# Two seventh token chunks, one per block, joined into one wide output group

## The chip, the core and the metric

The kernel runs on one core of a Trainium2 chip. Its engines work side by side, each through its own queue in program order: TensorE multiplies matrices (its weight loads are listed apart), VectorE and ScalarE do elementwise work and empty the accumulators (PSUM), GpSimd does elementwise work on SBUF and issues the loads, SyncE issues the stores. They wait for each other through semaphores. The metric is the device time of one execution in microseconds (us): 421.94 us for the kernel before, as the median of three runs.

## The reference

The inputs are q, k and v of shape (8, 12, 448, 64) and the three weights of a gated feed-forward block. In numpy:

```python
attn = softmax(q @ k.T / 8) @ v            # per batch and head
x    = attn.transpose(0, 2, 1, 3).reshape(3584, 768)
g    = x @ w_gate                          # 768 -> 1536
val  = x @ w_val
out  = (g * sigmoid(g) * val) @ w_out      # 1536 -> 768, float32
```

Everything before the final output is held in float16 on the chip, with float32 accumulation.

## The kernel before

**Blocks.** The 3584 tokens fall into four groups of two batches, 896 tokens each (`kk` = 0 to 3). While attention runs, the feed-forward work of groups 0 and 1 fills TensorE between attention's products. Groups 2 and 3 are put off to the end. They are the last two stages of the kernel, called here the first and the second put-off block. Each has two parts.

**The hidden part (`Unit`, L883, and `unit_items`, L1400).** The activations `hts` have the layout [128, 12 feature blocks, 896 tokens], in one buffer that both put-off blocks use in turn. A unit makes two feature blocks of gate (even unit `u`) or value (odd `u`) for all 896 tokens by a Strassen-Winograd scheme: seven products P1 to P7 of three matmuls each, instead of eight. Sums of the weights come from GpSimd (`weight_sums`, L873) and sums of the tokens from VectorE. A1 and A2 are ScalarE copies; D1 and D2 are VectorE additions (L964 and L968); F00, F01, F10 and F11 are the four outputs. For a value unit the F's run on VectorE (L982) and write `hts`: F00 and F10 write tokens 0 to 447 of the lower and the upper feature block of the pair, F01 and F11 write tokens 448 to 895. There are 12 units, `u` = 0 to 11.

**The output part (`OutPair`, L770).** A group of 896 tokens has seven chunks of 128. Chunks 0 to 5 form three pairs. `wide` (L800) computes a pair's 256 output rows by seven products again: a pair's activations are split into x and y (its two chunks) and into the lower and upper six feature blocks, so a11 and a12 are the halves of x, a21 and a22 those of y. Each product is six matmuls of 384 columns, with weights from `wo` or their sums `Tsum`. The products are taken in this order: a11; a21 + a22; s2; a12; s3; s4; a22. The four sums come from `h_sums` (L588 to L598) on VectorE: s3 = a11 - a21 (L593); a21 is overwritten by a21 + a22 (L594); s2 = a21 - a11 (L595); s4 = a12 - s2 (L596). Each of the four handles 128x768 elements. s2, s3 and s4 lie in one of three places, `Hall[0]` to `Hall[2]`. `add_sum` pops the next sum from a list, four during each `wide`, so that each pair's sums run during the pair before it. The first pair of a block has no pair before it, so its four sums are items of the hidden part (H0 to H3).

Chunk 6 has no partner. `single_out` (L1108) computes it plainly: 12 feature blocks times two halves of the output columns, 24 matmuls of 384 columns (items O0_0 to O1_11), a ScalarE copy per half (L1114) and a store per half.

**What sets the order.** `order_of` (L44) plans each put-off block. Items have an engine, a cost in us and a list of items that must be done. The planner repeatedly takes the engine whose next item can start first, and of that engine's items that can start within 0.12 us of that moment the one that stands first in the list. Instructions are emitted in that order, and each engine runs its own in the order of emission. The O and H items stand last in the list. After the planned items come the three `wide` calls of the block (`run_wide`, L1467), and after the first block's three pairs the second block's plan.

**Buffers.** `vraw` held the v inputs. Seen flat as `vfree`, its slots 6 to 8 (`vfree[:, 6 * VE :]`, 1536 elements per partition) hold one of the first put-off block's token sums (t6[1], which P6 reads) until that block's units are done. GpSimd's last work is the weight sums of unit 11.

Of the kernel before, what the change touches and what calls it, by code (L numbers as in the profile page):

```python
# [10 lines left out]
FP32 = mybir.dt.float32  # L11
FP16 = mybir.dt.float16
AF = mybir.ActivationFunctionType
# [3 lines left out]
HS = 4096.0  # L17
# [22 lines left out]
PE_, ACT_, DVE_, POOL_ = "PE", "ACT", "DVE", "POOL"  # L40
# [25 lines left out]
def kernel(  # L66
# [10 lines left out]
    nc = tc.nc  # L77
    B, H, S, D = q.shape
# [5 lines left out]
    NFB = DF // 128  # L84
# [5 lines left out]
    OH = DM // 2  # L90
# [23 lines left out]
    ps_f = ctx.enter_context(tc.tile_pool(name="ps_f", bufs=2, space=PSUM))  # L114
# [24 lines left out]
    NH = NFB // 2  # L139
# [12 lines left out]
    def hview(lo, n):  # L152
        return hall[:, ds(lo * NFB, n * NFB)].rearrange("p (f t) -> p f t", t=n)

    wo_all = consts.tile([128, 2, NFB, OH], FP16, name="wo")
    wo = [wo_all[:, i] for i in range(2)]
# [428 lines left out]
            lambda: nc.vector.tensor_sub(t4, b21, t2),  # L585
        ]

    def h_sums(hts, t, at, eng=nc.vector, f0=0, n=NH):  # L588
        lo, hi, x, y = ds(f0, n), ds(NH + f0, n), ts(2 * t, 128), ts(2 * t + 1, 128)
        a11, a12, a21, a22 = hts[:, lo, x], hts[:, hi, x], hts[:, lo, y], hts[:, hi, y]  # L590
        s2, s3, s4 = (h[:, lo] for h in Hall[at])
        return [
            lambda: eng.tensor_sub(s3, a11, a21),  # L593
            lambda: eng.tensor_add(a21, a21, a22),  # L594
            lambda: eng.tensor_sub(s2, a21, a11),  # L595
            lambda: eng.tensor_sub(s4, a12, s2),  # L596
        ]

    class Step:
        def __init__(self, kk, c0, n, hts, fb, late=None):  # L600
            self.at, self.hts, self.fb, self.late = (kk, c0, n), hts, fb, late
            self.t1 = None
            self.split = self.alone = False
            self.time = NCB * n / 2400.0
# [101 lines left out]
    def store(osb, kk, l0, n, m0, w, queues=(nc.sync,), large_first=False):  # L706
        parts = []
        l = l0
        while l < l0 + n:
            b, j = divmod(l, S)  # L710
            turned = D if b + NB * kk < QUAD // NHP else 0
            c, p0 = divmod((j + turned) % S, P)
            m = min(P - p0, l0 + n - l, (MQ if turned and j < MQ else S) - j)
            dst = out[ts(NB * kk + b, S), :].rearrange("(p c) m -> c p m", c=NC)[c, p0 : p0 + m]
            parts.append((m, dst[:, ds(m0, w)], osb[l - l0 : l - l0 + m, ds(m0, w)]))
            l += m
        if large_first:
            parts.sort(key=lambda part: -part[0])
        for x, (_, dst, src) in enumerate(parts):
            queues[x % len(queues)].dma_start(dst, src)  # L720
# [25 lines left out]
    def new_osb():  # L746
        return fp.tile([128, DM], FP32, tag="osb", bufs=4, name="osb")
# [21 lines left out]

    class OutPair:  # L770
        def __init__(self, kk, c0, hts, t, at=None, last=False):
            self.kk, self.c0, self.hts, self.t, self.last = kk, c0, hts, t, last
            self.at = t if at is None else at
            self.x, self.y = ts(2 * t, 128), ts(2 * t + 1, 128)
            self.osb = None

        def sums(self):
            return h_sums(self.hts, self.t, self.at)

        def hh(self, half, z):  # L780
            return lambda n: self.hts[:, half * NH + n, z]

        def hs(self, m):
            return lambda n: Hall[self.at][m][:, n]
# [10 lines left out]
            return self.osb  # L795

        def stored(self, z, lo=0, w=DM, queues=(nc.sync,)):
            store(self.osb[z], self.kk, self.c0 + (2 * self.t + z) * 128, 128, lo, w, queues, self.last)

        def wide(self, keep, add_sum, ns=(1, 2, 1), units=()):  # L800
            osb = self.open()
# [202 lines left out]
    with tc.manual_schedule():  # L1004
# [46 lines left out]
        sums = []  # L1051
# [52 lines left out]
        def token_space(flat, w):  # L1104
            n = min(4, flat.shape[1] // (NK * w))
            return [flat[:, ts(j, NK * w)].rearrange("p (c q) -> p c q", c=NK) for j in range(n)]

        def single_out(op, kk, c0, hts, ch, half, f):  # L1108
            nc.tensor.matmul(  # L1109
                op, lhsT=hts[:, f, ts(ch, 128)], rhs=wo[half][:, f], start=f == 0, stop=f == NFB - 1  # L1110
            )
            if f == NFB - 1:
                osb = new_osb()
                nc.scalar.activation(osb[:, ts(half, OH)], op, AF.Copy, scale=1.0 / HS)  # L1114
                store(osb, kk, c0 + ch * 128, 128, half * OH, OH)

        def add_sum(n=1):
            for _ in range(n):
# [77 lines left out]
        for kind in OPENING:  # L1196
            n = nth[kind]
# [29 lines left out]
        last = len(units)  # L1227
        while g < last or queue:
            n = 2 if g < WIDE * NC else 3
# [29 lines left out]
        vfree = vraw[:].rearrange("p s h c d -> p (s h c d)")  # L1259
        VE = 2 * NC * D  # L1260
# [4 lines left out]
        for x, (chunks, todo) in enumerate(plan):  # L1265
# [73 lines left out]
            if 0 < base - x <= len(FIRST_STEPS):  # L1339
                n = FIRST_STEPS[x - base]  # L1340
# [99 lines left out]
        def run_items(items):  # L1440
            items = {n: (e, t, [a for a in after if a in items], fn) for n, (e, t, after, fn) in items.items()}
            for name in order_of(items):
                items[name][3]()

        hts = hview(0, NT)

        def units_of(kk, t, last):
            units = {}
            items = unit_items(units, lambda u: Unit(u, S, X[kk], t, hts), S)
            pairs = [OutPair(kk, 0, hts, p, p if last else p % 2, last and p == 2) for p in range(3)]  # L1450
            ops = []

            def single_last(half, f):
                if not f:
                    ops.append(ps_f.tile([128, 512], FP32, tag="f", name="op")[:, 0:OH])
                single_out(ops[half], kk, 0, hts, 6, half, f)

            for half in range(2):
                for f in range(NFB):
                    after = [f"F{f % 2}1_{f // 2 * 2 + 1}", f"O{half}_{f - 1}" if f else f"F10_{NFB - 2 + half}"]  # L1460
                    items[f"O{half}_{f}"] = (PE_, OH / 2400 + 0.0025, after, lambda half=half, f=f: single_last(half, f))
            for m, fn in enumerate(pairs[0].sums()):
                u = NFB - 1 if m else NH - 1
                items[f"H{m}"] = (DVE_, 0.65, [f"F00_{u}", f"F10_{u}"] + [f"H{m - 1}"] * (m > 0), fn)
            return items, pairs

        def run_wide(pairs):  # L1467
            for n, pair in enumerate(pairs):
                pair.wide(kept[2 * (n % 2) : 2 * (n % 2) + 2], add_sum)

        items, pairs = units_of(KL - 1, t6, False)
        p0 = NPAIR - 1
        pv_open(p0, True)
# [11 lines left out]
            items[f"W_{u}"] = (POOL_, 3.65, [f"W_{u - 1}"], lambda u=u: weight_sums(u))  # L1485
        run_items(items)

        t7 = token_space(xp.tile([128, NCB, NT], FP16, tag="X", name="T")[:].rearrange("p a b -> p (a b)"), S)
        sums.clear()
        sums.extend(f for pair in pairs[1:] for f in pair.sums())  # L1490
# [4 lines left out]
        for t in qk16s:  # L1495
            flat = t[:].rearrange("p t c h d -> p (t c h d)")
            Hall[2].append(flat[:, 0 : NH * 128].rearrange("p (c f) -> p c f", c=NH))
        items, pairs = units_of(KL, t7, True)
        run_items(items)

# [32 lines left out]
```

## Time and profile before

| what | us |
|---|---|
| three runs, median (lowest, highest) | 421.94 (421.89, 422.28) |
| the profiled execution, its own time | 421.66 |
| its span, first to last instruction | 419.9 |
| TensorE busy / VectorE / ScalarE / GpSimd | 413.5 / 270.0 / 247.8 / 224.4 |
| first put-off block: last unit's last product begins, wide pairs begin | 318.94, 323.08 |
| second put-off block: the same | 391.36, 395.50 |
| the 24 matmuls of one chunk 6: 2 before the last product, 22 after it | 0.33 + 3.58 |
| one wide pair (42 matmuls), from pair to pair in the second block | 6.83 |

Times in the profile are microseconds from the span's start. A line of the timeline gives start, duration, engine, source line, operation, the tensors out<-in, shapes and a count; in brackets stands how long the engine had been idle and what released it. Matmuls are pipelined: a 384-column matmul is listed with 326 ns but the next one starts 0.1625 us after it, a 448-column one with 352 ns and 0.189 us. L numbers are lines of the kernel above; `un` and `ub` are the accumulators of the hidden part, `op` those of chunk 6, `og` and `ob` those of the wide pairs.

### The profile page before, as it was taken

How to read it: one execution, taken by the hardware profiler on the slowest of the kernel's cores; microseconds unless marked ns; L12 is line 12 of the kernel's file. 1: busy time of each engine (PE TensorE's matmuls, PEld its weight loads, DVE VectorE, ACT ScalarE, POOL GpSimd, SP SyncE). 2: the span in 40 equal slices, each digit the busy share in tenths (PEclk: the TensorE clock that was granted, in tenths of full speed). 3: DMA queues.
4: the chain of work that ended last, by engine and by line, in shares of the span. 5: the costliest groups of instructions: out<-in, count | busy, mean ns of one | idle time of the engine just before them, and what ended most of it. 6: DMA issues, size and time to landing. Idle time of an engine off the chain costs nothing.

```text
span 419.9 us, 10841 instructions
## 1 busy us (share of the span) xinstructions
PE 413.5 (98%) x4340; PEld 259.5 (62%) x4340; DVE 270.0 (64%) x614; ACT 247.8 (59%) x386; POOL 224.4 (53%) x343
## 2 busy tenths in 40 slices
PE   8999999999999999999999999999999999999996
PEld 3666666655567786787768676545555655555564
DVE  4767562785687784676746568665755665665563
ACT  6975667656677675787647676645453125555221
POOL 8656624997798986497987806599700000000000
PEclk9999999999999999999999999999999999999999
DMA  8999999999999999999999734600001240000125
GB/s 133 188 200 200 200 174 195 144 154 196 180 185 138 147 219 175 153 152 161 152 179 164 105 72 90 186 14 0 2 0 30 85 118 33 0 2 0 39 75 152
DMA packets 108467, 50.29 MB, mean 120 GB/s; under 512 B 60416, under 2 KB 105344, under 8 KB 108416
## 3 DMA queue, kind: packets, MB, share of 16 engines
q0 software_dynamic: 46800, 24.56, 49.3%
q1 hardware_dynamic: 61344, 24.79, 33.5%
q8 instruction: 34, 0.56, 0.6%
q10 hardware_dynamic: 272, 0.25, 0.2%
q14 instruction: 17, 0.14, 0.1%
HBM read 49.55 MB, written 11.01 MB: 144 GB/s over the span
## 4 chain that ended last, share of the span: by engine, by line
PE 94%; DVE 2%; ACT 1%; DMA 1%; issue 1%; SPq 0%; DVEq 0%
PE gp L610 14%; PE un L915 12%; PE vp L610 12%; PE og L759 10%; PE ub L915 10%; PE acc L462 8%; PE ob L759 8%; PE s L356 5%; PE op L732 4%; PE s L393 2%; PE acc L426 2%; PE op L1109 2%; PE s L368 1%; PE tp L324 1%; ACT E L403 1%; DMA rk<-in_k_dram 1%
## 5 line engine op out<-in xcount | busy, mean ns | idle before, releaser
L378 ACT ACTIVATE E<-s 128x896 f16<-128x896 f32 x126 | 107.5, 917 | 37.4 <-PE s L356 27.3
L610 PE MATMUL gp<-X,wg 128*128 128x256 f16 (+3 forms) x396 | 61.7, 302 | 0.0
L610 PE MATMUL vp<-X,wv 128*128 128x256 f16 (+3 forms) x396 | 58.6, 291 | 0.0
L180 POOL DMA_DIRECT2D vraw<-in_v_dram x72 | 43.9, 632 | 18.1 <-DMA wo<-in_moe_w_out_dram 8.3
L240 POOL COPY qk<-qkraw 128x512 f16<-128x512 f16 x70 | 43.0, 661 | 18.7 <-DMA qkT<-qk 18.2
L610 PEld LDWEIGHTS <-wv 128*128 128x128 f16 x438 | 41.1, 98 | 15.2 <-DVE xt L505 0.2
L180 POOL DMA_DIRECT2D qkraw<-in_k_dram x70 | 42.6, 625 | 5.2 <-DMA wo<-in_moe_w_out_dram 3.4
L403 ACT ACTIVATE E<-s 112x896 f16<-112x896 f32 x48 | 40.6, 917 | 7.5 <-PE s L393 7.5
L610 PEld LDWEIGHTS <-wg 128*128 128x128 f16 x396 | 34.9, 98 | 16.2 <-issue 2.2
L462 PEld LDWEIGHTS <-E 128*128 128x128 f16 (+2 forms) x1224 | 38.1, 98 | 9.1 <-issue 3.9
L462 PE MATMUL acc<-vo,E 128*128 128x65 f16 (+2 forms) x1224 | 42.1, 193 | 0.6 <-DVE osb L816 0.3
L759 PEld LDWEIGHTS <-hts 128*128 128x128 f16 x270 | 25.9, 98 | 16.0
L690 DVE SCALAR_TENSOR_TENSOR t<-sg,gp 128x384 f32<-128x384 f32 (+1 forms) x30 | 18.0, 615 | 24.0 <-ACT sg L637 23.8
L696 DVE SCALAR_TENSOR_TENSOR hts<-t,vp 128x256 f16<-128x256 f32 (+3 forms) x66 | 30.7, 465 | 3.4 <-PE vp L610 1.2
L505 DVE TENSOR_TENSOR xt<-acc,R 128x256 f16<-128x256 f32 x72 | 30.6, 425 | 2.5
L203 POOL DMA_DIRECT2D qkraw<-in_q_dram x43 | 29.4, 684 | 4.0 <-DMA vraw<-in_v_dram 1.1
L356 PE MATMUL s<-qkT 64*64 64x448 f16 (+1 forms) x288 | 28.8, 352 | 0.0
L980 ACT ACTIVATE silu<-un 128x448 f32<-128x448 f32 x24 | 13.0, 543 | 22.4 <-PE un L915 21.8
L964 DVE TENSOR_TENSOR un<-ub,kept 128x448 f32<-128x448 f32 x24 | 15.1, 630 | 16.1 <-ACT kept L961 10.3
L759 PE MATMUL og<-wo,hts 128*128 128x384 f16 x132 | 25.0, 326 | 0.0
L968 DVE TENSOR_TENSOR kept<-ub,kept 128x448 f32<-128x448 f32 x24 | 15.0, 625 | 14.7 <-PE ub L915 14.7
L221 DVE COPY vo<-vraw 128x512 f16<-128x512 f16 (+1 forms) x48 | 21.1, 440 | 2.9 <-DMA vraw<-in_v_dram 2.9
(210 smaller groups left out, 735.4 us busy)
## 6 DMA issues: line engine op xcount, KB each, us to landing
vraw<-in_v_dram POOLq DMA_DIRECT2D x72, 64.0 KB, 5.3
qkraw<-in_q_dram POOLq DMA_DIRECT2D x39, 112.0 KB, 4.9
qkraw<-in_k_dram POOLq DMA_DIRECT2D x68, 64.0 KB, 5.1
wg<-in_moe_w_gate_dram POOLq DMA_DIRECT2D x8, 288.0 KB, 10.2
wv<-in_moe_w_val_dram POOLq DMA_DIRECT2D x8, 288.0 KB, 10.5
wo<-in_moe_w_out_dram POOLq DMA_DIRECT2D x2, 1152.0 KB, 18.7
out_dram<-osb SPq DMA_DIRECT2D x7, 288.0 KB, 3.5
out_dram<-osb SPq DMA_DIRECT2D x9, 192.0 KB, 3.2
```

Of the source, the lines that this page charges most:

```text
L180: eng.dma_start(dst[ts(s, 64)], rows)
L203: nc.gpsimd.dma_start(dst, flat.rearrange("h (p c) d -> p h (c d)", c=NC))
L240: nc.gpsimd.tensor_copy(dst.rearrange("p c h d -> p h c d"), src)
L356: nc.tensor.matmul(s[ts(half, m), hx, 0:S].rearrange("p (c q) -> p c q", q=P), lhsT=t[ts(hx, 64), ds((c + low(pr, hx)) * 128 + half * m, m ...
L378: nc.scalar.activation(e, s[:, :, 0:S], AF.Exp, scale=sm_scale)
L403: nc.scalar.activation(e[:, :, 0:S], s[0:P, :, 0:S], AF.Exp, scale=sm_scale)
L462: nc.tensor.matmul(acc[ds(lo, m), ts((j + pr % 2) % (KR + 1), D + 1)], lhsT=e[rows, ds(hx * S + j * 128 + lo, m)], rhs=Vts[pr % NV][rows, ...
L505: nc.vector.tensor_tensor(xt[:, :, hx], a4[:, :, 0:D], r[:].unsqueeze(2).to_broadcast([128, KR + 1, D]), ALU.mult,)
L610: nc.tensor.matmul(dst[:, 0:w], lhsT=wslice(kind, self.fb, cb), rhs=X[kk][:, cb, ds(c0 + lo, w)], start=(cb == 0), stop=(cb == NCB - 1),)
L696: nc.vector.scalar_tensor_tensor(self.hts[:, self.fb, ds(lo, w)], self.t1[:, ds(lo, w)], 0.5 * HS, vp[:, 0:w], ALU.mult, ALU.mult)
L759: nc.tensor.matmul(dst, lhsT=lhs(n), rhs=rhs(n), start=first and n == 0, stop=n == NH - 1, skip_group_check=True)
L915: mm = nc.tensor.matmul(dst, lhsT=lhs[:, n], rhs=rhs[:, n], start=first and n == 0, stop=n == NK - 1, skip_group_check=True,)
```

## The change

Chunk 6 of neither block is computed alone any more. When the first put-off block's units are planned and emitted, GpSimd copies its chunk 6 (all 12 feature blocks, 128x1536 elements) from `hts` into the free slots of `vraw` (`apart_chunk`). The second block then has four wide groups: its first pair, a mixed group with x = the kept chunk and y = its own chunk 6, and its other two pairs. The mixed group's two output tiles go to the rows of their own blocks. The mixed group's sums run during the first pair's `wide`, like any pair's; the third place for sums, used by the last pair before, now belongs to the pair of chunks 2 and 3, and the last pair uses the first place.

In both put-off blocks the first pair's sums H1 to H3 are planned in two parts: feature blocks 0 to 3 of each half ("e", which need the F's up to unit 9) and 4 to 5 ("l", which need unit 11). H0 stays whole. The removed O items leave the plan without TensorE work behind the last product.

```diff
-    def h_sums(hts, t, at, eng=nc.vector, f0=0, n=NH):
-        lo, hi, x, y = ds(f0, n), ds(NH + f0, n), ts(2 * t, 128), ts(2 * t + 1, 128)
-        a11, a12, a21, a22 = hts[:, lo, x], hts[:, hi, x], hts[:, lo, y], hts[:, hi, y]
+    def h_sums(x, y, at, eng=nc.vector, f0=0, n=NH):
+        lo, hi = ds(f0, n), ds(NH + f0, n)
+        a11, a12, a21, a22 = x[:, lo], x[:, hi], y[:, lo], y[:, hi]
...
     class OutPair:
         def __init__(self, kk, c0, hts, t, at=None, last=False):
-            self.kk, self.c0, self.hts, self.t, self.last = kk, c0, hts, t, last
-            self.at = t if at is None else at
-            self.x, self.y = ts(2 * t, 128), ts(2 * t + 1, 128)
+            self.last, self.at = last, t if at is None else at
+            self.rows = [(kk, c0 + (2 * t + z) * 128) for z in range(2)]
+            self.x, self.y = (hts[:, :, ts(2 * t + z, 128)] for z in range(2))
...
-            pairs = [OutPair(kk, 0, hts, p, p if last else p % 2, last and p == 2) for p in range(3)]
-            ops = []
...
-            for half in range(2):
-                for f in range(NFB):
-                    after = [f"F{f % 2}1_{f // 2 * 2 + 1}", f"O{half}_{f - 1}" if f else f"F10_{NFB - 2 + half}"]
-                    items[f"O{half}_{f}"] = (PE_, OH / 2400 + 0.0025, after, lambda half=half, f=f: single_last(half, f))
-            for m, fn in enumerate(pairs[0].sums()):
-                u = NFB - 1 if m else NH - 1
-                items[f"H{m}"] = (DVE_, 0.65, [f"F00_{u}", f"F10_{u}"] + [f"H{m - 1}"] * (m > 0), fn)
+            pairs = [OutPair(kk, 0, hts, p, p % 2, last and p == 2) for p in range(3)]
+            if last:
+                mixed = OutPair(kk, 0, hts, 0, 1)
+                mixed.x, mixed.y = apart_chunk, hts[:, :, ts(6, 128)]
+                mixed.rows = [(kk - 1, 6 * 128), (kk, 6 * 128)]
+                pairs.insert(1, mixed)
+                pairs[2].at = 2
+            items["H0"] = (DVE_, 0.65, [f"F00_{NH - 1}", f"F10_{NH - 1}"], pairs[0].sums()[0])
+            for part, f0, n, u in (("e", 0, 4, NFB - 3), ("l", 4, 2, NFB - 1)):
+                for m, fn in enumerate(pairs[0].sums(f0, n)[1:], 1):
+                    after = [f"F00_{u}", f"F10_{u}", "H0"] + [f"H{m - 1}{part}"] * (m > 1)
+                    items[f"H{m}{part}"] = (DVE_, 0.07 + 0.1 * n, after, fn)
             return items, pairs
...
         run_items(items)
 
+        apart_chunk = vfree[:, 6 * VE :].rearrange("p (f t) -> p f t", t=128)
+        nc.gpsimd.tensor_copy(apart_chunk, hts[:, :, ts(6, 128)])
         t7 = token_space(xp.tile([128, NCB, NT], FP16, tag="X", name="T")[:].rearrange("p a b -> p (a b)"), S)
```

More of the change, by code (lines that the diff above doesn't have):

```diff
@@ L771, in __init__, with sums @@
         def __init__(self, kk, c0, hts, t, at=None, last=False):
-            self.kk, self.c0, self.hts, self.t, self.last = kk, c0, hts, t, last
-            self.at = t if at is None else at
-            self.x, self.y = ts(2 * t, 128), ts(2 * t + 1, 128)
+            self.last, self.at = last, t if at is None else at
+            self.rows = [(kk, c0 + (2 * t + z) * 128) for z in range(2)]
+            self.x, self.y = (hts[:, :, ts(2 * t + z, 128)] for z in range(2))
             self.osb = None
-        def sums(self):
-            return h_sums(self.hts, self.t, self.at)
+        def sums(self, f0=0, n=NH):
+            return h_sums(self.x, self.y, self.at, f0=f0, n=n)
         def hh(self, half, z):
-            return lambda n: self.hts[:, half * NH + n, z]
+            return lambda n: z[:, half * NH + n]
         def hs(self, m):
@@ L797, in stored @@
         def stored(self, z, lo=0, w=DM, queues=(nc.sync,)):
-            store(self.osb[z], self.kk, self.c0 + (2 * self.t + z) * 128, 128, lo, w, queues, self.last)
+            store(self.osb[z], *self.rows[z], 128, lo, w, queues, self.last)
         def wide(self, keep, add_sum, ns=(1, 2, 1), units=()):
@@ L1106, in token_space @@
             return [flat[:, ts(j, NK * w)].rearrange("p (c q) -> p c q", c=NK) for j in range(n)]
[L1108 to L1115, printed above, removed]
         def add_sum(n=1):
@@ L1449, in units_of @@
             items = unit_items(units, lambda u: Unit(u, S, X[kk], t, hts), S)
-            pairs = [OutPair(kk, 0, hts, p, p if last else p % 2, last and p == 2) for p in range(3)]
-            ops = []
[L1453 to L1456, printed above, removed]
-            for half in range(2):
-                for f in range(NFB):
-                    after = [f"F{f % 2}1_{f // 2 * 2 + 1}", f"O{half}_{f - 1}" if f else f"F10_{NFB - 2 + half}"]
-                    items[f"O{half}_{f}"] = (PE_, OH / 2400 + 0.0025, after, lambda half=half, f=f: single_last(half, f))
-            for m, fn in enumerate(pairs[0].sums()):
-                u = NFB - 1 if m else NH - 1
-                items[f"H{m}"] = (DVE_, 0.65, [f"F00_{u}", f"F10_{u}"] + [f"H{m - 1}"] * (m > 0), fn)
+            pairs = [OutPair(kk, 0, hts, p, p % 2, last and p == 2) for p in range(3)]
[10 more added lines that the diff above has]
+                    items[f"H{m}{part}"] = (DVE_, 0.07 + 0.1 * n, after, fn)
             return items, pairs
```

## The prediction

> **What bounds the kernel now.** I read the page first (engine shares), then the chain of waits over the last 100 us, then the timeline at the end of each put-off block, and last the places where GpSimd and VectorE work at the same moment.
>
> ```profile
> span 419.9 us, 10841 instructions
> PE 413.5 (98%) x4340; PEld 259.5 (62%) x4340; DVE 270.0 (64%) x614; ACT 247.8 (59%) x386; POOL 224.4 (53%) x343
> ...
> POOL 8656624997798986497987806599700000000000
> ```
>
> TensorE is busy 98% of the span, so a matmul taken out is time gained as long as nothing leaves TensorE waiting in its place. GpSimd is idle in the last 11 of 40 slices. The chain of waits at the end of the first put-off block:
>
> ```profile
> 318.78 0.33 PE op L1109 x2
> 319.10 0.57 PE ub L915 x3
> 319.67 3.58 PE op L1109 x22
> 323.24 1.95 PE og L759 x12
> ```
>
> It names TensorE alone: three matmuls of the last unit's last product, P4_11 (`ub`), with two chunk-6 matmuls ahead of them and 22 behind. What these 24 cover shows in the timeline of that place:
>
> ```profile
> 318.25 0.62 DVE L968 TENSOR_TENSOR kept<-ub,kept 128x448 f32<-128x448 f32 x1
> ...
> 318.61 0.49 PE L1109 MATMUL op<-wo,hts 128*128 128x384 f16 x2
> ...
> 318.94 0.73 PE L915 MATMUL ub<-qkraw,wv 128*128 128x448 f16 x3
> 318.98 0.62 DVE L982 SCALAR_TENSOR_TENSOR hts<-silu,kept 128x448 f16<-128x448 f32 x1
> ...
> 319.51 3.74 PE L1109 MATMUL op<-wo,hts 128*128 128x384 f16 x22
> 319.52 0.61 DVE L982 SCALAR_TENSOR_TENSOR hts<-silu,un 128x448 f16<-128x448 f32 x1
> 320.05 0.61 DVE L982 SCALAR_TENSOR_TENSOR hts<-silu,ub 128x448 f16<-128x448 f32 x1
> 320.70 0.56 DVE L594 TENSOR_TENSOR hts<-hts 128x768 f16<-128x768 f16 x1
> 321.29 0.56 DVE L595 TENSOR_TENSOR hsum<-hts 128x768 f16<-128x768 f16 x1
> 321.88 0.56 DVE L596 TENSOR_TENSOR hsum<-hts,hsum 128x768 f16<-128x768 f16 x1
> ```
>
> P4_11 overwrites the accumulator that D2_11 (L968) reads until 318.87. Then VectorE runs F11, F01, F10 and the sums H1 to H3, up to 322.44, while TensorE works on chunk 6. The second block repeats this to 0.01 us, 72.42 us later. How fast TensorE follows VectorE, and what GpSimd does to VectorE:
>
> ```profile
> 274.09 0.62 DVE L964 TENSOR_TENSOR un<-ub,kept 128x448 f32<-128x448 f32 x1
> 274.76 0.73 PE L915 MATMUL ub<-qkraw 128*128 128x448 f16 x3 [0.33 <-DVE un L964]
> ...
> 296.50 0.90 POOL L880 TENSOR_TENSOR xt<-wg 128x384 f16<-128x384 f16 x1
> 296.86 0.96 DVE L593 TENSOR_TENSOR hsum<-hts 128x768 f16<-128x768 f16 x1
> ```
>
> TensorE starts 0.05 us after the VectorE operation it waits for (274.09 + 0.62 to 274.76). A group sum (L593), 0.55 us elsewhere, takes 0.96 us beside a GpSimd operation: it ends at 297.82, so it began in effect at 297.27, 0.13 before that operation's listed end of 297.40. A GpSimd copy does the same: one of `qk` ends at 140.94, and the L596 sum that starts under it at 140.47 takes 0.89 us and ends at 141.36, 0.55 after 140.81. The operations with one SBUF input are not held (L982 with `ub` at 296.21: 0.61 us under a GpSimd operation).
>
> **The change part by part.**
>
> *Matmuls.* 2 x 24 of chunk 6 go, 42 of the mixed group come. Six fewer at 0.1625 us (3.58 / 22): **-0.975 us**. The mixed group's sums, copies and stores lie as any pair's do: a pair takes 6.83 us of TensorE with about 4.4 of VectorE (eight operations of 0.55) and 1.5 of ScalarE. SyncE's queue gets four full-width stores for the mixed group instead of eight half-width ones in the two blocks; none is the kernel's last, and an output tile comes round again two pairs later, as now. Priced at nothing.
>
> *Ahead of P4_11.* Its cover of two matmuls goes. P3_11's last matmul leaves the queue at 318.61; P4_11 can start at 318.87 + 0.05 = 318.92. That is 0.30 us idle, in each block: **+0.61**. Bounds: 0.26 (no delay behind VectorE) to 0.33 (what the two matmuls took) each.
>
> *The early sums.* The planner, worked through with its own costs, puts H1e and H2e after D1_10 and H3e after D2_10, where VectorE sits idle 1.08 and 0.58 us in the trace. Their length: 768 elements take 0.55 us and 1344 take 0.85, so a straight line gives 0.42 for 512 and 0.29 for 256. H1e follows D1_10, which ends at 314.33, and H2e ends at 314.33 + 0.42 + 0.03 + 0.42 = 315.20; D2_10 starts at 315.41. H3e follows D2_10 (316.03) and ends at 316.45; D1_11 starts at 316.61. Hidden; if halving saved nothing (0.55 each), H2e would end 0.05 us too late.
>
> *The late sums, second block.* TensorE now goes from P4_11 straight into the first pair: P4_11 3 x 0.189, a11 6 x 0.1625, then a21 + a22, whose first four matmuls need only H1e. The fifth is due 0.57 + 0.97 + 0.65 = 2.19 us after P4_11's start (391.29, D2_11's end here, + 0.05 = 391.34), at 393.53. H1l follows F10 as H1 does now, 393.12 to 393.41. The weight load waits for it, 0.05 later, and the matmul follows its load by 0.16: 393.62. **+0.09** (0 to 0.36, the latter if H1l takes 0.55). H2l and H3l end before their products.
>
> *The late sums, first block.* Here GpSimd's copy waits for F01 (the last writer of chunk 6), which ends at 320.13, before F10 does. GpSimd has followed VectorE by 0.11 us (226.18 to 226.29), so it starts at 320.24, 0.46 ahead of H1l. F10 reads one input from PSUM and is not held; H1l reads two from SBUF and is. The copy's length is in no row: 512 elements take 0.613 at best, a memset of one element takes 0.10, so 1536 take 0.10 + 3 x 0.513 = 1.64; the bounds are 1.38 (if the 0.231 of a 128x128 memset were all fixed) and 1.84 (three times 0.613). I take 1.6, near the first. H1l then starts at 320.24 + 1.6 - 0.13 = 321.71, ends at 322.00, and the fifth matmul goes at 322.21 instead of 318.92 + 2.19 = 321.11: **+1.10** (0.88 to 1.34 by the copy's bounds; 0.09 if the copy misses H1l). Behind H1l stand H2l, H3l and the p15 combination (L825); all come before their products. Nothing follows the copy on GpSimd's queue, and the second block's first write to chunk 6 comes over 25 us later.
>
> The Trainium skill, SBUF — State Buffer, section "SBUF: two separate sides", says that VectorE operations with two SBUF inputs and reading GpSimd operations take a shared port pair by an exclusive lock for the whole instruction. The rows agree for instructions up to 0.9 us (0.96 against 0.55 us); no run here shows one of 1.6 us. By the rule the sum stands; with a port handed over in between, it would be 1.0 us less. The same skill, GPSIMD Engine Reference, section "3.1 Elementwise — side-by-side cycle accounting", gives 1.03 cycles per element for simple bodies: an estimate by that page of 0.613 + 1024 x 0.86 ns = 1.49 us, and a sum 0.1 us lower.
>
> *Sum.* -0.975 + 0.61 + 0.09 + 1.10 = **+0.82 us**. The profiled execution took 421.66 us (1.76 around its span of 419.9), 0.28 under the median of the runs; on the median, 421.94 + 0.82 = **422.75 us**. The case's own range goes by the copy's bounds and the other terms': +0.5 to +1.3.
>
> **The rivals.**
>
> *Slower: short sums cost what long ones do.* Place: H1l, in both blocks. If a 256-element sum took 0.55, it would come 0.26 later in both: +0.82 + 0.53 = +1.35, 423.3 us. For it: dependent sums follow each other with gaps of 0.03. Against: 0.55 and 0.85 lie on a line whose fixed part is 0.15. From 0.30 us per late sum on, the total passes 0.2%.
>
> *The copy misses the sums.* If GpSimd starts over 0.5 us after F01, H1l goes first. If the copy then enters between H1l and H2l, H2l ends near 322.6 where its product's fifth matmul is due at 322.18: about +0.5 in all. If it enters later or holds nothing, the sum is -0.975 + 0.61 + 0.18 = -0.19, 421.75 us. For it: GpSimd has been idle for 18 us there. Against: the 0.11 above, and the held copy row.
>
> *Faster: the whole gain arrives.* 420.96 us, if something else covers P4_11 and H1l. Against: the plan holds no TensorE item that could go there.
>
> **How the numbers follow.** The forecast has 0.62, the slower rival 0.10, the missed sums 0.20 (half of it at -0.2), the whole gain 0.04; 0.04 is left for worse than 423.3. From 421.6 (below the missed case) to 423.2 (the copy at its long end) about 0.2 is left out. A change of 0.2%, 0.84 us, is about what can be told from no change here; the forecast passes it when the copy takes over 1.63 us, so I halve it: slower 0.31 + 0.10 + 0.02 = 0.43, faster 0.05, within 0.52.
>
> **What would show it.** Right: `op` gone from the two tails, and four groups of `og` and `ob` matmuls in the second block; TensorE idle 0.3 us ahead of P4_11 in both blocks, released by L968; a GpSimd copy near 320.2 of about 1.6 us; L594's late part in the first block listed with over 1 us, and about 1.1 us TensorE idle behind it; 0.1 in the second block. Wrong: L594 late parts alike in both blocks, a copy well below 1.3 us or starting behind 320.7, or D2_10 late.

## The result and the profile after

The changed kernel takes 423.48 us (median of 22 runs), the kernel before 422.51 us (22 runs beside them). The ratio is 1.0025 [1.0015, 1.0034], that is +1.06 us (0.63 to 1.44; the two medians are 0.97 apart): slower, and a little more so than the forecast of +0.82. The forecast's 422.75 us stood on a median of three runs, 421.94, which 22 runs moved to 422.51.

The page of the kernel after, its first lines and GpSimd's slices:

```profile
span 423.7 us, 10837 instructions
PE 414.3 (98%) x4334; PEld 259.0 (61%) x4334; DVE 274.8 (65%) x628; ACT 247.5 (58%) x385; POOL 224.5 (53%) x344
...
POOL 8656615998986885498966905599701000000000
```

Six matmuls fewer, fourteen VectorE operations more, and one GpSimd operation more, in slice 31, where GpSimd was idle before. The profiled execution itself took 425.49 us, the longest of the 22; its span is 3.8 us above that of before. Most of this is not the change. From the first instruction to the start of the first put-off block's last D1 (L964) lie 319.41 us here and 316.61 before; in the ten kernels tried below the same stretch takes 316.58 to 320.48, although only four of them touch it (six matmuls more or fewer in the warm-up). So everything below is measured from that D1 to the end of the span. That tail takes 103.27 us before and 104.31 after: **+1.04**, which agrees with the timed +1.06. Up to the end of the last VectorE operation it is 100.01 and 100.40 (**+0.40**, taken before rounding, as are the differences below), from there to the end of the span 3.27 and 3.91 (**+0.64**). Both parts count. They are read from one profiled execution of each kernel; up to the last VectorE operation, kernels with the same work there agree to 0.01 (100.40 in after, e2 and e9; 99.64 in e1, e4 and e7).

**The first block's end.** The chain of waits of the kernel after, where before TensorE alone stood (start, us, what):

```profile
319.87 0.58 PE un L915 x3
320.45 0.02 issue
320.47 0.62 DVE hts L982
321.09 0.58 DVE kept L968
...
322.84 0.63 DVE hts L982
323.47 0.02 issue
323.49 1.12 DVE hts L594
324.61 0.05 issue
324.65 0.50 PE og L759 x2
```

Two new links: D2_11 (L968) releases the last product, and H1l (L594) releases two matmuls of the second product. The timeline there, 2.80 us later than the same places of before:

```profile
321.04 0.62 DVE L968 TENSOR_TENSOR kept<-ub,kept 128x448 f32<-128x448 f32 x1
...
321.72 0.73 PE L915 MATMUL ub<-qkraw,wv 128*128 128x448 f16 x3
...
322.31 0.61 DVE L982 SCALAR_TENSOR_TENSOR hts<-silu,un 128x448 f16<-128x448 f32 x1
...
322.84 0.62 DVE L982 SCALAR_TENSOR_TENSOR hts<-silu,ub 128x448 f16<-128x448 f32 x1
322.99 1.46 POOL L1477 COPY vraw<-hts 128x1536 f16<-128x1536 f16 x1 [18.00 <-DVE hts L982]
323.26 0.81 PE L759 MATMUL og<-E,hts 128*128 128x384 f16 x4
323.49 1.10 DVE L594 TENSOR_TENSOR hts<-hts 128x256 f16<-128x256 f16 x1
...
324.65 0.50 PE L759 MATMUL og<-E,hts 128*128 128x384 f16 x2 [0.58 <-DVE hts L594]
```

P3_11's last matmul is out at 321.41 and P4_11 starts at 321.72: 0.31 idle. GpSimd's copy starts 0.07 after F01's end (322.31 + 0.61) and takes 1.46. H1l, listed with 1.10, ends at 324.59. A free 256-element sum takes 0.29, so it ran in effect from 324.30, which is 0.15 before the copy's listed end of 324.45. The second product's fifth matmul, due at 321.72 + 2.19 = 323.91, starts at 324.65: **+0.74**.

**The second block's end**, where no copy runs:

```profile
391.31 0.73 PE L915 MATMUL ub<-T,wv 128*128 128x448 f16 x3
...
392.85 1.14 PE L759 MATMUL og<-E,hts 128*128 128x384 f16 x6
393.08 0.29 DVE L594 TENSOR_TENSOR hts<-hts 128x256 f16<-128x256 f16 x1
```

P4_11 again starts 0.31 late (its predecessor was out at 391.00), but the six matmuls of the second product follow without a break: H1l costs nothing here. So the body's sum is -0.975 + 2 x 0.31 + 0.74 + 0.00 = +0.385, against 0.40 measured.

**The kernel's end.** The last wide pair's stores go out in five steps, each with one issue on SyncE and one on ScalarE. Their issues (L720; ns min/median/max), in the kernel before and in the kernel after:

```profile
L720 SPq DMA_DIRECT2D out_dram<-osb x5: 316/322/393, 413.8 to 416.8; - x5
L720 ACTq DMA_DIRECT2D out_dram<-osb x5: 376/379/390, 413.8 to 416.8; - x5
```

```profile
L720 SPq DMA_DIRECT2D out_dram<-osb x5: 317/376/522, 417.0 to 420.1; - x5
L720 ACTq DMA_DIRECT2D out_dram<-osb x5: 376/383/513, 417.0 to 420.2; - x5
```

The second pair takes 0.52 and 0.51 us, on both queues at once; before, none takes over 0.39. ScalarE's next copy (L843) stands behind its own issue, so all later stores go out 0.13 to 0.15 later. The last data is later by more than that: it has landed 2.73 us after the end of the last VectorE operation, and 2.33 before. A second thing differs: SyncE waits at the very end for the eight semaphores that the stores count up, in a fixed order. When the waits are satisfied, in us after the end of the last VectorE operation (read from the trace, the first nine; the first of them is for a semaphore of the loads):

```
before  0.59 0.66 0.72 1.54 1.64 1.98 2.04 2.25 2.35
after   0.72 2.41 2.47 2.64 2.75 2.81 2.87 2.93 2.99
```

Before, most waits are over before the last data lands. After, the second wait already belongs to one of the last stores, and the rest follow it one by one, some 0.06 us each where nothing else holds them. From the last wait to the end of the span it is 0.92 in both. So of the +0.64, 0.40 is data that lands later and 0.24 the waits that are still open behind it (0.26 against 0.02). The stores take the eight semaphores in turn, and the change leaves 58 on SyncE's queue instead of 62: the last stores meet other semaphores.

### The profile page after: what moved, and what is told of

Read it like the earlier page. It is cut to its first block, busy times and chain, and to the rows that moved or that the text cites. A ratio compares the mean times of both kernels' runs of the same rounds, so it can differ in the third digit from the quotient of the medians.

```text
span 423.7 us, 10837 instructions
## 1 busy us (share of the span) xinstructions
PE 414.3 (98%) x4334; PEld 259.0 (61%) x4334; DVE 274.8 (65%) x628; ACT 247.5 (58%) x385; POOL 224.5 (53%) x344
## 4 chain that ended last, share of the span: by engine, by line
PE 87%; DVE 7%; DMA 2%; issue 2%; ACT 1%; POOL 0%; SPq 0%; DVEq 0%; POOLq 0%
PE gp L610 12%; PE un L915 12%; PE og L759 11%; PE vp L610 11%; PE ub L915 9%; PE ob L759 8%; PE acc L462 7%; PE s L356 5%; PE op L732 3%; PE s L393 3%; PE acc L426 2%; DMA qkT<-qk 1%; PE tp L324 1%; PE s L368 1%; PE wp L166 1%
## 5 line engine op out<-in xcount | busy, mean ns | idle before, releaser
L240 POOL COPY qk<-qkraw 128x512 f16<-128x512 f16 x70 | 42.1, 652 | 27.4 <-DMA qkT<-qk 26.2
L759 PEld LDWEIGHTS <-hts 128*128 128x128 f16 x282 | 26.9, 98 | 17.8 <-DVE hts L594 1.1
L964 DVE TENSOR_TENSOR un<-ub,kept 128x448 f32<-128x448 f32 x24 | 15.1, 630 | 15.4 <-ACT kept L961 10.3
L968 DVE TENSOR_TENSOR kept<-ub,kept 128x448 f32<-128x448 f32 x24 | 15.0, 625 | 13.1 <-PE ub L915 13.1
L957 ACT ACTIVATE ub<-un 128x448 f32<-128x448 f32 x24 | 12.7, 529 | 16.4 <-PE un L915 13.9
```

The lines of the kernel that those rows point to most:

```text
L240: nc.gpsimd.tensor_copy(dst.rearrange("p c h d -> p h c d"), src)
L759: nc.tensor.matmul(dst, lhsT=lhs(n), rhs=rhs(n), start=first and n == 0, stop=n == NH - 1, skip_group_check=True)
```

## The experiments

Ratios are to the kernel before beside them. "Body" and "end" are the two parts of the tail defined above; differences of a few tenths are read from them, since the timed intervals are about as wide as that. The expectations are as written before each run. In the order in which they follow, the questions were: is the +0.74 the copy's hold; is the end's +0.64 the number of stores; what else the end depends on; and what fills the two gaps that are left.

**e1: the copy behind the late sums.** A small GpSimd copy of H3l's result stands ahead of the big one, which so waits until H1l to H3l are through; one operation is added.

```diff
+        nc.gpsimd.tensor_copy(apart_chunk[:, 0], Hall[0][2][:, NH - 1])
         nc.gpsimd.tensor_copy(apart_chunk, hts[:, :, ts(6, 128)])
```

> The changed kernel, with GpSimd's copy of chunk 6 held back until the late sum H3l is written (a 128x128 copy out of H3l's result goes ahead of it). The tail is counted from the start of the first put-off block's last D1 addition to the end of the span: 103.27 us before, 104.30 changed. Theory A, the tail's own account (-0.98 matmuls, +0.62 ahead of P4_11, +0.74 late sum held by the copy, +0.64 between the last VectorE operation and the end of the span): H1l takes 0.29 us instead of 1.10, TensorE's stall behind it goes, the tail is 103.56 us, and the time is +0.3 us against the kernel before. Theory B, the cause lies ahead of the tail, where the profiled execution of the changed kernel is 2.79 us late: the time stays at +1.0 us whatever the tail does.

The timeline at the first block's end:

```profile
322.32 0.29 DVE L594 TENSOR_TENSOR hts<-hts 128x256 f16<-128x256 f16 x1
...
323.40 0.29 POOL L1477 COPY vraw<-hsum 128x128 f16<-128x128 f16 x1 [19.58 <-DVE hsum L596]
...
323.75 1.47 POOL L1478 COPY vraw<-hts 128x1536 f16<-128x1536 f16 x1
...
324.71 0.92 DVE L593 TENSOR_TENSOR qkraw<-hts 128x768 f16<-128x768 f16 x1
```

H1l takes 0.29, the body 99.64: 0.76 less than after. That the copy's hold on H1l costs 0.74 to 0.76 us is shown. The copy now holds an L593 sum instead (0.92 against 0.55), which nothing waits for yet. But the time is 1.0011 [0.9999, 1.0023] and the end 4.26 us, 0.36 worse than after; its second pair of issues takes 0.93 and 0.92.

**e2: 62 stores again.** The mixed group's four stores become eight half-width ones, as chunk 6 had before.

```diff
...
+        def stored_whole(self, z):
+            w = OH if self.halved else DM
+            for lo in range(0, DM, w):
+                self.stored(z, lo, w)
...
-                self.stored(1)
+                self.stored_whole(1)
...
+                mixed.halved = True
```

> The changed kernel, with the mixed group's two output tiles stored in half widths, so that SyncE issues 62 output stores again instead of 58 and the end of the kernel waits for the same semaphores in the same order as before. Theory A (the order of the last waits): 3.27 us from the last VectorE operation to the end of the span instead of 3.91, a tail of 103.66 us, +0.4 us against the kernel before. Theory C (the last stores land later by chance or for their own sake): 3.9 us stay, the tail stays at 104.3.

Measured: ratio 1.0006 [0.9997, 1.0015], body 100.40, end 3.78, tail 104.18. The number of stores alone doesn't bring the end back. The second pair of issues is now even longer, 0.78 and 0.77 us. The timed runs don't confirm the size: they give +0.25 us (-0.13 to 0.63) over the kernel before where this tail gives +0.91, and the profiled execution, 423.04, was among the longest of the eleven (422.28 to 423.10). So the held issues are shown for that execution; whether the others have them is not shown.

**e3: 58 stores in the kernel before.** Chunk 6's two halves share one output tile and one store.

```diff
+        osb6 = [None]
...
-                osb = new_osb()
-                nc.scalar.activation(osb[:, ts(half, OH)], op, AF.Copy, scale=1.0 / HS)
-                store(osb, kk, c0 + ch * 128, 128, half * OH, OH)
+                if not half:
+                    osb6[0] = new_osb()
+                nc.scalar.activation(osb6[0][:, ts(half, OH)], op, AF.Copy, scale=1.0 / HS)
+                if half:
+                    store(osb6[0], kk, c0 + ch * 128, 128, 0, DM)
```

> The kernel before, with each chunk 6 stored once at full width instead of twice at half width: 58 stores, as in the changed kernel, and nothing else. Theory A: 3.9 us from the last VectorE operation to the end, a tail of 103.9 us, +0.6 us (0.15%). Theory C: as the kernel before, 3.27 and 103.27 us, no change in time.

Measured: 1.0007 [0.9996, 1.0019], end 3.52: +0.26 over before and not +0.64, with all issues as short as before and the last data packet through at the same time (1.90 us after the last VectorE operation, 1.92 before). The waits run 0.58, 2.01, 2.07, 2.24, and so on: the changed order of the semaphores is worth about a quarter of a microsecond, and something else the rest.

**e4: e1 and e2 together.**

> The changed kernel with both: the copy held behind H3l and the mixed group's stores in half widths. Theory A: a tail of 102.92 us, 0.35 us less than the kernel before. Theory B: still about 1 us slower. Theory C: a tail of 103.6 us, +0.3 us.

Measured: 0.9997 [0.9987, 1.0008], body 99.64 as expected, end 3.90 instead of 3.27. The second pair of issues took 0.92 and 0.91.

**What the stretched issues share.** A DMA queue of its own (q8, kind "instruction") carries packets of 16 KB. There are 34 of them in each of these kernels, against 8668 matmuls and weight loads in the kernel after, one for about 255; so they are taken here for TensorE's instruction fetches, which the tests with more and fewer TensorE instructions below bear out. The last one does not lie at the same place against the end in all kernels. In the DMA view of the kernel after, in the stretch from 417.0 to 418.0, it stands beside the first 27 packets of the stores' data:

```profile
q1 hardware_dynamic: 27, 0.04, 14.9%
q8 instruction: 1, 0.02, 6.2%
```

If TensorE asks for it after a fixed number of its instructions, then the twelve that the change has taken out (six matmuls, each with its weight load) move it towards the end, by about the 0.98 us that six matmuls take; it moved by 1.28. All times in us from the end of the last VectorE operation; the second pair is issued at -1.67 in every kernel, and SyncE's issue is given (read from the traces):

```
kernel   fetch starts  has landed  issue takes  issue ends   end
before       -3.80        -2.78        0.32        -1.35     3.27
e3           -3.82        -2.87        0.32        -1.35     3.52
after        -2.52        -1.53        0.52        -1.15     3.91
e2           -2.34        -1.28        0.78        -0.89     3.78
e4           -2.42        -1.14        0.92        -0.76     3.90
e1           -2.41        -1.13        0.93        -0.74     4.26
```

In the four kernels where the fetch lands after -1.67, SyncE's issues end 0.38 to 0.39 us after its landing. The data of the pair ahead is late as well. That first pair is issued at -2.83 (e3: -2.92), before the fetch starts in these four. Its store on SyncE lands 1.14 or 1.15 us after the fetch has landed (at -0.39 in after, up to 0.02 in e1), and at -0.86 and -0.95 in before and e3. The theory that the table gave: the missing TensorE instructions moved the fetch into the last stores. It is tested by adding twelve back where they cost nothing, and by taking twelve out of the kernel before (e7 to e10). Two runs ahead of them measured the plan's own gaps.

**e5: the first pair's sums whole**, as before, in the changed kernel.

```diff
...
-            for part, f0, n, u in (("e", 0, 4, NFB - 3), ("l", 4, 2, NFB - 1)):
...
+            for m, fn in enumerate(pairs[0].sums()):
+                u = NFB - 1 if m else NH - 1
+                items[f"H{m}"] = (DVE_, 0.65, [f"F00_{u}", f"F10_{u}"] + [f"H{m - 1}"] * (m > 0), fn)
```

> The changed kernel with the group sums H1 to H3 whole again (768 elements per partition, all after unit 11). If the split is what keeps TensorE's wait short, the second product of the first pair now waits for its first matmul already: second block, H1 ends 0.56 us behind 393.08, the product is due 0.57 + 0.97 us after P4_11's start: a stall of 0.9 us instead of none. First block, H1 waits for the copy's end as before and then takes 0.56: a stall of 1.7 us instead of 0.74. From the first block's last D1 to the last VectorE operation 102.2 us instead of 100.4. If the split does not matter: 100.4 as in the changed kernel.

One execution. The timeline of the first block's end:

```profile
320.59 1.47 POOL L1475 COPY vraw<-hts 128x1536 f16<-128x1536 f16 x1 [17.99 <-DVE hts L982]
321.09 1.38 DVE L594 TENSOR_TENSOR hts<-hts 128x768 f16<-128x768 f16 x1
...
322.52 1.15 PE L759 MATMUL og<-E,hts 128*128 128x384 f16 x6 [1.51 <-DVE hts L594]
```

The body is 102.18, 1.78 us above after: so much is the split worth. Without it all six matmuls wait, not two, until 322.52, which is 1.67 after P4_11 and a11 would have let them start (319.31 + 1.54), against 0.74 in after; in the second block they start at 392.21 instead of 391.36, 0.85 late. The two make the 1.78. The end is 4.33, and it fits the table: the fetch starts at -2.42 and lands at -1.09, the second pair takes 0.97 and 0.96, and SyncE's issue ends 0.39 after the landing.

**e6: the two gaps filled.** Two matmuls of the first pair's a11 product go ahead of P4_11, in the place of the two of chunk 6, and F01_11 (the last writer of chunk 6, so what the copy waits for) is planned behind H3l; e2's stores too.

```diff
...
+            e, us, after, fn = items[f"F01_{NFB - 1}"]
+            items[f"F01_{NFB - 1}"] = (e, us, after + ["H3l"], fn)
+            for n in range(2):
+                after = [f"P3_{NFB - 1}"] + ["A0"] * n
+                items[f"A{n}"] = (PE_, OH / 2400 + 0.0025, after, lambda: pairs[0].first(1))
```

> The changed kernel with three edits: the mixed group's stores in half widths; F01 of unit 11 planned behind the late sums, which puts F10 and the late sums 0.3 to 0.5 us earlier and the copy, which waits for F01, behind them; and two of the first pair's six a11 matmuls planned ahead of P4_11, where the chunk-6 matmuls stood. The tail's account: no idle time ahead of P4_11, at most 0.1 us at the late sum in each block; from the first block's last D1 to the last VectorE operation 100.01 - 0.98 + 0.2 = 99.2 us at most (100.01 before, 99.64 with the copy held). If TensorE's wait ahead of P4_11 only moves to the late sum: 99.6.

One execution: body 99.04, 0.96 us below the kernel before. The whole gain of six matmuls (0.975) arrives once nothing waits. The end was 3.38: the fetch began only at -1.82, the second pair of issues kept its 0.32, and the last pair came late instead (0.37 and 0.55 after the last VectorE operation, not 0.15 and 0.23). The trace shows why that pair: the ten stores take eight semaphores in turn, so the last two use those of the first two and wait until these have landed. They landed at 0.31 and 0.48 here, 0.06 ahead of the issues, and at -0.86 and -0.68 in the kernel before. SyncE's is 1.18 after the fetch's landing (-0.87), nearly as in the four kernels of the table: here the fetch held data that was already issued, and no issue.

**e7: e4 with twelve TensorE instructions more.** Six matmuls of 8 columns, each with its weight load, join the warm-up at the kernel's start, where TensorE waits for the first loads.

```diff
...
+        for _ in range(tiny):
+            nc.tensor.matmul(wp[:, 0:8], lhsT=warm[:], rhs=warm[:, 0:8], start=True, stop=True)
...
-        dummy(1, 2)
+        dummy(1, 2, 6)
```

> The version with the held copy and half-width stores, with six 8-column matmuls more among the warming matmuls at the very start, so that TensorE has as many instructions as in the kernel before. Theory D: TensorE's 16 KB instruction fetch, which the twelve instructions fewer have moved from 3.8 to 2.5 us ahead of the last VectorE operation's end, holds up the last stores' issue on SyncE and ScalarE (0.78 and 0.92 us instead of 0.32). Then the fetch is back at 3.8, the store issues take 0.32, and 3.3 us pass from the last VectorE operation to the end instead of 3.9: a tail of 102.9 us, 0.35 under the kernel before. If the stores are late for another reason, 3.9 and a tail of 103.5 stay.

Measured: 0.9990 [0.997, 1.001], tail 102.92, body 99.64, end 3.28 (3.90 in e4). The last stores' issues:

```profile
L722 SPq DMA_DIRECT2D out_dram<-osb x5: 317/322/390, 413.7 to 416.7; - x5
L722 ACTq DMA_DIRECT2D out_dram<-osb x5: 375/382/391, 413.8 to 416.8; - x5
```

They are as short as before, with the fetch at -4.35. Nothing after the warm-up differs from e4, so the end's 0.62 came from those twelve instructions, and the place of the fetch is what they are seen to move.

**e8: e6 with the same twelve.**

> The three edits of the filled version and the six small matmuls at the start together. By all the accounts above: at most 99.2 us from the first block's last D1 to the last VectorE operation and 3.3 us from there, a tail of 102.4 us, 0.8 us (0.2%) less than the kernel before. If theory D fails, 3.9 us at the end and 0.2 us less.

Measured: 421.92 us, 0.9976 [0.9957, 0.9994] of the kernel before, tail 102.34 (0.93 below before), body 99.05, end 3.29. The interval lies 0.25 to 1.8 us below the kernel before, so it is faster than that one and, by way of it, than the changed kernel. Its first block's end:

```profile
319.41 0.62 DVE L988 TENSOR_TENSOR kept<-ub,kept 128x448 f32<-128x448 f32 x1
...
319.78 0.49 PE L810 MATMUL og<-wo,hts 128*128 128x384 f16 x2
...
320.11 0.73 PE L935 MATMUL ub<-qkraw,wv 128*128 128x448 f16 x3
...
321.32 1.14 PE L761 MATMUL og<-E,hts 128*128 128x384 f16 x6
...
321.60 0.29 DVE L596 TENSOR_TENSOR hts<-hts 128x256 f16<-128x256 f16 x1
...
323.19 1.47 POOL L1503 COPY vraw<-hts 128x1536 f16<-128x1536 f16 x1 [19.82 <-PE og L761]
```

P4_11 goes at 320.11, straight behind two a11 matmuls, when D2_11 has ended (320.03). The late sum takes 0.29 and nothing waits for it, and the copy comes 1.3 us after it.

**e9: the changed kernel with the twelve, and nothing else.**

> The changed kernel with the six 8-column matmuls at the start alone; the copy is not held and the stores are 58. It parts the two causes at the end. Theory D (the instruction fetch): the last stores' issues take 0.32 to 0.38 us again. What is left over the kernel before is the order of the last waits, 0.26 us as in the kernel before with 58 stores (3.52 against 3.27): 3.5 us from the last VectorE operation to the end, 100.4 to it, a tail of 103.9 us, +0.65 us against the kernel before. If 12 instructions more do nothing here: 3.9 and 104.3.

Measured: tail 103.95, body 100.40, end 3.55, issues of at most 0.39 us, with the fetch at -3.68. So the twelve instructions, and with them the fetch, are worth 0.35 in the changed kernel, and 0.29 over before is left: e3's order of waits. The timing, 1.0027 [1.0015, 1.0039] from seven runs, doesn't resolve this 0.35.

**e10: the kernel before with twelve TensorE instructions fewer.** Six of the warm-up's matmuls are left out; the rest is untouched.

```diff
-        dummy(7)
+        dummy(1)
```

> The kernel before with six of the eight warming matmuls at the start left out, so that TensorE has 12 instructions fewer, as in the changed kernel; nothing else. Theory D: the 16 KB instruction fetch comes near 2.5 us ahead of the last VectorE operation's end instead of 3.8, the store issues that begin 1.67 us ahead of it take 0.5 to 0.9 us instead of 0.32 and 0.38, and 3.5 to 3.9 us pass from the last VectorE operation to the end instead of 3.27, with no change to the tail's body (100.01). If the fetch is innocent: 3.27. The start may change by some tenths, since TensorE is warmed less.

One execution. The last stores' issues:

```profile
L720 SPq DMA_DIRECT2D out_dram<-osb x5: 317/374/572, 417.7 to 420.8; - x5
L720 ACTq DMA_DIRECT2D out_dram<-osb x5: 376/379/564, 417.7 to 420.9; - x5
```

The fetch now starts at -2.43 and lands at -1.48, the second pair takes 0.57 and 0.56, and the end 3.59 instead of 3.27, with 62 stores and the old plan. The first pair's store on SyncE again lands 1.15 after the fetch. The collision is made in the kernel before by nothing but six matmuls fewer at its start. (Its whole time, 425.85, isn't comparable: its start is 3.87 us longer.)

## Why the prediction was wrong

Its sign was right, its sum was too small, and the likeliest class, within 0.2%, was missed: the measured +0.25% lies in the 0.43 that was given to slower. The time lies above the range, whose upper end was 423.2. Two steps failed: the end of the kernel was priced at nothing and cost 0.64, and the first block's late sum was priced at 1.10 and cost 0.74. By its own steps:

- *Matmuls*, -0.975: right. e6 and e8 show it undisguised (body -0.96).
- *Ahead of P4_11*, 0.30 in each block: 0.31 twice.
- *The early sums hidden*: right. 512 elements take 0.41 to 0.43, 256 take 0.29, and D2_10 (L968 at 318.20) still finds VectorE idle for 0.30.
- *The late sums, second block*, +0.09: 0.00. The step added 0.16 from weight load to matmul; the fifth matmul came right behind the fourth.
- *The late sums, first block*, +1.10: the mechanism was right, the size was not: 0.74. Of the 0.36 too much, the copy was 0.14 (1.46, not 1.6), the weight load again 0.16, the copy's start 0.04 (0.07 behind F01, not 0.11) and the sum's start ahead of the copy's end 0.02. The estimate from the Trainium skill's GPSIMD Engine Reference, section "3.1 Elementwise — side-by-side cycle accounting", 1.49 us, was nearer than the value taken from the rows. The rule of the Trainium skill's SBUF — State Buffer, section "SBUF: two separate sides", that the port lock holds for the whole instruction, is borne out for one of 1.46 us: H1l ended as if it had begun only 0.15 before the listed end.
- *SyncE's queue, "Priced at nothing"*: this step failed. Four stores fewer changed the order in which the last waits are met, +0.26 to +0.29 (e3, e9), and twelve TensorE instructions fewer moved a fetch into the last stores, +0.33 to +0.35 (e10, e9), together the +0.64. The step looked at whether a store was late and whether a tile came free. It did not ask what the end of the kernel counts on, though the removed instructions and stores stood in the same paragraph.
- *On the median*: the three runs of before were on the low side by 0.57, as much as a term of the sum. On them even the right sum of +1.04 gives 422.98, inside the range, and on the 22 runs the forecast's +0.82 gives 423.33, outside it. So it is this median, and no term of the sum, that put the time outside.

Body alone, the forecast was +0.82 and the result +0.40. The end's +0.64 came on top, so two misses of opposite sign left the total only 0.2 apart; that closeness is luck.

Of the rivals, the short sums that cost what long ones do fell (0.29), and so did the copy that misses the sums (it starts 0.50 us ahead of H1l). That the whole gain arrives was held against the plan, which had no TensorE item to put there. The items existed, though: a11 needs only finished blocks of `hts`, and the planner was never given its matmuls. Of the signs listed, all of the "right" ones are there except the size of the idle time behind H1l (0.74, not 1.1) and the 0.1 of the second block.

## What to carry to other kernels

When an edit takes work off the bounding engine, list what that work covered and give the planner other ready work to put there, and let a long GpSimd copy wait for something behind the VectorE sums that share its port: in this kernel that is the difference between +0.40 and -0.96 us. For changes of a few tenths, price the end of the kernel as a stage of its own, with the last stores' issues, the order of the last waits, and where the instruction fetches fall. And measure from a fixed instruction to the end when the stretch before it varies by more than the effect.

## What the runs showed of the hardware

**An instruction fetch holds up the stores of two other engines.** In after, e1, e2, e4, e5 and e10 a pair of store issues on SyncE and ScalarE ends 0.37 to 0.39 us after TensorE's 16 KB fetch has landed, 0.51 to 0.97 us long instead of 0.32 and 0.38. In these six and in e6 the data of the pair issued before it lands late too: SyncE's store 1.14 to 1.18 us after the fetch. The fetch itself takes 0.95 to 1.37 us. Whether the issues wait for the fetch or for the data held behind it was not tried. That it is the fetch, and not something else that the twelve instructions move, rests on these fixed distances. Being under way at the same time is not enough: in e6 a fetch begins 0.15 us before the second pair, and in the kernel before one lands 0.05 after the first pair is issued, and neither pair's issues are held. The Trainium skill, Runtime: NRT & Kernel Launch, section "Instruction fetch mechanics", says that a 16 KB block is fetched while the current one runs and that its cost is mostly hidden. For TensorE that agrees: in the last 5 us of its work in the kernel after no gap between matmuls is over 0.06 us. For the stores of other engines the 0.33 to 0.35 us here are not hidden.

**Work at the start can move the end.** Six 8-column matmuls in the warm-up changed the last 3.5 us by 0.35 to 0.62 us (e9, e7), and shifted the last fetch by 1.2 to 1.9 us.

**A held VectorE sum runs from shortly before GpSimd's listed end.** H1l runs in effect from 0.15 us before the listed end of the copy, as a sum did from 0.13 before in the kernel before. Whether the copy is through by then or lists its end late isn't shown.
